# A planner that lengthens GpSimd and VectorE instructions beside each other, with a new load order, gates and ranks

## The chip, the cores and the metric

The kernel runs on one core of one Trainium2 chip. The metric is the device time of one execution in microseconds (us); lower is better. The kernel before took 287.44 us in the median of four runs (285.84 to 288.22). Besides, one execution was profiled; it took 286.84 us, of which the profile's span covers 284.9 us.

The engines appear in the profile as PE (TensorE matmuls), PEld (TensorE weight loads), DVE (VectorE), ACT (ScalarE), POOL (GpSimd) and SP (SyncE, which issues nearly all DMAs).

## The reference

Two layers follow each other. The first is a linear attention with a decaying state, over 4 batches, 8 heads, 768 steps and a head dimension of 48:

```python
for t in range(S):
    cur = np.einsum('bhd,bhe->bhde', u[None] * kt, vt)
    y[:, :, t] = np.einsum('bhd,bhde->bhe', rt, state + cur)
    state = w[None, :, :, None] * state + np.einsum('bhd,bhe->bhde', kt, vt)
```

Its result, reshaped to 3072 rows of 384, goes through a mixture of four experts, all of them computed for each row and weighted by normalised probabilities:

```python
for e in range(E):                       # 4 experts, 384 -> 1024 -> 384
    h = np.maximum(x @ w1[e], 0.0)
    out += p[:, e:e + 1] * (h @ w2[e])
```

## The kernel before

**Chunks and super-chunks.** The sequence is cut into chunks of 128 steps, 6 for each of the 4 batches, 24 in all, numbered `ci` with the batch running fastest. Four chunks (one of each batch) make a super-chunk `sc`, so there are six. A chunk's attention becomes a 128x128 masked product for each head (`At`, `mask`), a product with V (`Y`), a term of the state carried from the chunk before of the same batch, and an update of that state (`Sm`, `Sv`, `S`).

**The work of one chunk.** Three loads (`Rt`, `Kt`, `Vt`, 192 KB each, L232) go into one of four input buffers (`inp`). VectorE scales R and K by powers of the decay (`scale`, L397 from chunk 8 on). GpSimd multiplies R, K and u (`ruk_a`, L409, and `ruk_b`, L417), VectorE reduces that to a coefficient (`dcoef`, L430), and GpSimd multiplies V by it (`dv`, L435). A buffer comes free when scale, ruk_a, the cast of V and dv are done. From chunk 8 on, two DMA transposes per pair of chunks (L442) bring the scaled tile to the layout that TensorE wants; Y and dv are added on VectorE (`Yout`, L571); the state update is an add on VectorE (`Sv`, L638) and two half products on GpSimd (`S`, L648).

**The experts.** Super-chunks 0 and 1 go through eight slots `(expert, super-chunk, single)`: first layer (L701 or L707) into PSUM, relu on ScalarE (L716, L718), second layer (L738), weighted addition (L747, L749). For super-chunks 2 to 5, ScalarE scales the attention's result by each expert's probability first (`Xs`, L591) and DMA transposes it (L601); all four experts' first layers run (L707), and their hidden activations form one product of 2x2 blocks that is computed with seven block products (`P`, L905) in place of eight. This needs sums of the weight blocks (`mix`, L818) once, and sums of activation blocks (`sum`, L874) for each pair of chunks; products are collected by ScalarE copies (L932) and VectorE additions (`C`, L934). The mixes are computed once, after the two scaled super-chunks are through.

**The order.** Nothing is scheduled on the chip. While the program is built, a planner in Python plays the execution through. Every job has an engine, a duration, the jobs it needs, tokens that it takes and gives back (buffers), and a rank. Whenever an engine is free, the planner starts the ready job with the lowest rank. The order in which jobs start becomes the order of instructions in each engine's queue. The chip runs each queue strictly in that order, with semaphores for the dependences; the planner's times are thus not executed, only its order. Loads are SP jobs, ranked by their place in the list `ORDER`; one that has no free buffer is passed over for the next.

**What the change touches.** `GATES` (L140) names for each pair of chunks from 8 on an event before which it may not be scaled: a number below 8 is the first matmul of that slot, 8 to 11 the first matmul of an expert's first layer in super-chunk 2, 12 to 15 one of its block products, and from 16 on the same for super-chunk 3. `MIX_RANK`, `XS_RANK` and `SUM_RANK` shift the ranks of mixes, Xs and sums. `SLOWER` multiplies planned durations after the planner's 85th microsecond, by engine, for all but sum, Xs, mix and scale. `SHARED` lengthens a VectorE sum, scale, mix or Xs by 0.6 of the time for which GpSimd is still busy when it starts. `TAIL` is the time between an instruction's end and the start of one that waits for it.

Of the kernel before, what the change touches and what calls it, by code (L numbers as in the profile page):

```python
# [19 lines left out]
def kernel(  # L20
# [14 lines left out]
    B, H, S, D = r.shape  # L35
    HD = H * D
    C = 128
    NCH = S // C
    TOTC = B * NCH
    SUB = B  # L40
# [81 lines left out]
    for b in range(B):  # L122
# [14 lines left out]

    GATES = [3, 5, 8, 8, 16, 17, 7, 23]  # L140
    WARM, NSPIN = 6.6, 6
    TAIL = {"T": 0.27, "V": 0.17, "A": 0.20, "P": 0.17, "S": 0.0}
    DMAT = 8
# [6 lines left out]
    FIRST = 2  # L150
    SCALED = 2
    ONTO = {6: 1, 5: 6, 3: 5, 4: 7}
    MIX_RANK = 16.0
    XS_ON = {'A': 0.61}
    MIX_ON = {'V': 0.97}
    SCALE_US = 0.97
    VB_ON = {'A': 0.42, 'P': 0.5}
    XS_RANK = 0
    SUM_RANK = -60
    EARLY_SUM = 0.0  # L160
    NSH = 4
    SEQ_S = (((1, 0), (3, 0), (2, 0), (1, 1), (3, 1), (2, 1), (4, 0), (4, 1)),
             ((1, 2), (3, 2), (2, 2), (4, 2)))
    LATE, SLOWER = 85.0, {"V": 1.13, "P": 1.06, "A": 1.15}
    SHARED = 0.6
    SLOTS += [(e, sc, 0) for sc in range(2, SCALED) for e in range(E)]
    ORDER_P = (1, 2, 6, 7, 4, 5, 3)
    SEQ_P = ((0, 1, 0), (0, 2, 0), (0, 7, 0), (0, 1, 1), (0, 2, 1), (0, 7, 1), (0, 6, 0), (0, 6, 1), (0, 4, 0),
# [13 lines left out]
    def job(name, on, run, needs=(), rank=0.0, takes=(), drops=(), moves=None,  # L182
            behind=()):
        j = Job()
        j.behind = behind
        j.name, j.on, j.run, j.needs, j.rank = name, on, run, list(needs), rank
        j.takes, j.drops, j.moves = takes, drops, moves
        for k in drops:
            tokens[k] = tokens.get(k, 0) + 1
        j.pad = 0.0  # L190
        ci = name[1] if isinstance(name, tuple) and name[0] in ATT else -1
        if ci >= SUB:

            j.pad = PAD_PE if "T" in on else PAD
        j.no = len(jobs)
        assert name not in jobs
        jobs[name] = j
# [61 lines left out]
    def load_p():  # L259
# [1 line left out]
            prow, moe_domain_probs.rearrange("(n p) e -> n p e", p=C)))  # L261

    ORDER = ("K0 K1 R0 R2 R1 V0 K2 w1e0.1 w1e0.0 w1e0.2 V1 K3 V2 R3 w2e0.0 V3 w2e0.1 w2e0.2 p K4 w1e1.1 "
# [3 lines left out]
             " ".join(f"c{i}" for i in range(14, TOTC))).split()  # L267
    for what in ORDER:
        if what == "p":
            load_p()  # L270
# [93 lines left out]
    def attention(ci):  # L364
        b, c = ci % B, ci // B
# [3 lines left out]
        rk = float(ci)  # L369
        on_pe = -20.0 + 0.01 * ci  # L370
        pre = [("S", ci - NRK), ("T", ci - NRK, 1)] if ci >= NRK else []
        if ci >= 2 * SUB:

            g = GATES[(ci - 2 * SUB) // 2]
            if g < len(SLOTS):
                pre.append(("l1", *SLOTS[g][:2], 0, 0))
            else:
                i, g = divmod(g - len(SLOTS), 8)
# [16 lines left out]
        us = 0.48 if ci < SUB else 0.65  # L395
# [188 lines left out]
        elif dmat:  # L584
            n_p = b * NCH + c

            def xs(e):
                def run(eng):
                    o = y_e[:, e * HD:(e + 1) * HD]
                    if eng == "A":  # L590
                        nc.scalar.mul(o, tl["Ysb", ci], p_nat[:, e, n_p:n_p + 1])  # L591
                    else:
                        nc.vector.tensor_scalar(o, tl["Ysb", ci], scalar1=p_nat[:, e, n_p:n_p + 1],
                                                scalar2=None, op0=ALU.mult)
                return run
            for e in range(E):
                job(("Xs", ci, e), XS_ON, xs(e), [("Yout", ci)] + all_cast, rk + XS_RANK,
                    ((f"Yse{e // 2}", ci),) if e % 2 == 0 else (), (("dv", ci),),
# [54 lines left out]
        if c == 0:  # L653
            job(("S", ci), {"V": 0.56}, sv, [("Sm", ci), ("Yout", SUB - 1)], rk + 2, (), (("ys", "S", ci),))
        else:
            job(("Sv", ci), {"V": 0.5}, sv, [("Sm", ci)], rk - 0.1, (("Tn", ci),), (("ys", "S", ci),))
            job(("S", ci), {"P": 1.3}, sp, [("Sv", ci)], rk - 0.5, (), (("Tn", ci),))

    y_sb = weights.tile([128, 3 * HD], BF16)
    y_free, y_at = [0, 1, 2], {}  # L660
# [136 lines left out]
    def mix(what, hf):  # L797
# [28 lines left out]
        if not where:  # L826
            needs += [("l2", e, ci) for ci in range(SCALED * SUB) for e in (2 * hf, 2 * hf + 1)]
            needs += [("l2s", ci, e) for ci in range(SCALED * SUB, FIRST * SUB) for e in (2 * hf, 2 * hf + 1)]
        job(("mix", what, hf), MIX_ON, run, needs, MIX_RANK, ((where, "mix", home),) if where else ())

# [14 lines left out]
    def products(sc, q, at0):  # L845
# [21 lines left out]
        def sum_job(k, hf):  # L867
# [10 lines left out]
            if k in (2, 4):  # L878
                needs += [("P", sc, q, 1 if k == 2 else 2, h) for h in hs]
            job(("sum", sc, q, k, hf), {"V": 1.23 if hf == 2 else 0.7}, run, needs,  # L880
                at_of[{1: 6, 3: 6, 2: 6, 4: 3}[k]] + (EARLY_SUM if k in (1, 3) and not q and not hf else SUM_RANK), tuple(s_tok[h] for h in hs) if k == 1 else (),
                tuple(x for h in hs for x in hts[h]) + (tuple(s_tok[h] for h in hs) if k in (1, 2) else ()),
# [121 lines left out]
    avail = {"T": 3.7, "V": 4.5, "A": 3.3, "P": 1.5, "S": 0.6}  # L1004
# [25 lines left out]
    events = []  # L1030
    started = []
    gone = set()
    unknown = {n: len(q) for n, q in left.items()}
    known = {n: 0.0 for n in left}
    soon = {e: [] for e in avail}
# [2 lines left out]
    def offer(j):  # L1038
        for e in j.on:
            heapq.heappush(waiting[e], (j.rank, j.no, j))  # L1040
# [5 lines left out]
    now, seq, n_done = 0.0, 1, 0  # L1046
# [7 lines left out]
    def start(e):  # L1054

        nonlocal seq
        put_back, got = [], None
        while waiting[e]:
            it = heapq.heappop(waiting[e])
            j = it[2]  # L1060
            if j.name in gone:
                continue
            if ready_at[j.name] <= now + 1e-9 and \
                    fits(j) and \
                    not (j.moves and queued and queued[-1][1] > now + BACKLOG):
                got = j
                break
            put_back.append(it)
        for it in put_back:
            heapq.heappush(waiting[e], it)  # L1070
        if got is not None and now < HURRY:

            us = got.on[e]
            for i in soon[e]:
                if i.name not in gone and i.rank < got.rank and fits(i) and                         now < known[i.name] < now + 0.6 * us:
                    heapq.heappush(waiting[e], (got.rank, got.no, got))
                    heapq.heappush(events, (known[i.name], seq, "eng", e))
                    seq += 1
                    return False
        if got is None:  # L1080
            return False
        j = got
        gone.add(j.name)
        for t in j.takes:
            if t not in held:
                held.add(t)
                free[t[0]] -= 1
        us = j.on[e] * (2.0 if e == "T" and now < WARM and j.name not in ("wmm", "umm") else 1.0)
        if e in SLOWER and now > LATE and j.name[0] not in ("sum", "Xs", "mix", "scale"):
            us *= SLOWER[e]  # L1090
        if e == "V" and now > LATE and j.name[0] in ("sum", "scale", "mix", "Xs"):
            us += SHARED * min(us, max(0.0, avail["P"] - now))
        if j.moves:
            taken, end = dma(now, us, *j.moves)
            us = taken - now + 0.04
        started.append((now, len(started), e, j))
        avail[e] = now + us
        if not j.moves:
            end = now + us + TAIL[e]
        heapq.heappush(events, (avail[e], seq, "eng", e))  # L1100
        heapq.heappush(events, (end, seq + 1, "done", j))
        for u2 in users.get(j.name, ()):
            unknown[u2.name] -= 1
            known[u2.name] = max(known[u2.name], end)
            if not unknown[u2.name] and end < HURRY + 5:
                for e2 in u2.on:
                    soon[e2].append(u2)
        seq += 2
        return True

    while n_done < len(jobs):
        assert events, "no job can begin"
        now, _, what, x = heapq.heappop(events)
        batch = [(what, x)]
        while events and events[0][0] <= now + 1e-9:
            _, _, what, x = heapq.heappop(events)
            batch.append((what, x))
        for what, x in batch:
            if what == "done":
                n_done += 1  # L1120
                for t in x.drops:
                    count[t] -= 1
                    if count[t] == 0:
                        free[t[0]] += 1
                for u2 in users.get(x.name, ()):
                    left[u2.name].discard(x.name)
                    if not left[u2.name]:
                        ready_at[u2.name] = now + u2.pad
                        offer(u2)
                        if u2.pad:  # L1130
                            for e2 in u2.on:
                                heapq.heappush(events, (now + u2.pad, seq, "eng", e2))
                                seq += 1
        for e in avail:
            if avail[e] <= now + 1e-9:
                start(e)
# [49 lines left out]
```

## Time and profile before

| What | Value |
|---|---|
| median of four runs | 287.44 us |
| lowest, highest | 285.84, 288.22 us |
| the profiled execution, its span | 286.84 us, 284.9 us |
| TensorE busy with matmuls | 277.5 us (97%) |
| ScalarE, VectorE, GpSimd busy | 186.8, 179.3, 106.2 us |
| sums, mixes and scales of two chunks' R and K on VectorE (L874, L818, L397) | 45.4 + 7.5 + 16.6 us |
| GpSimd: ruk_a and ruk_b, dv, S | 27.1 + 25.6, 21.8, 22.0 us |
| HBM read, written | 26.79 MB, 4.72 MB |

A busy time is the union of an engine's instructions. Matmuls are pipelined: a 128x512 one is shown as 379 ns long, and the next one's start tells the true pace. An engine's idle time costs nothing unless what it does next ends on the path to the last store.

### The profile page before, as it was taken

What the parts mean: (1) busy time and instruction counts of PE and PEld (TensorE: products, weight loads), DVE (VectorE), ACT (ScalarE), POOL (GpSimd) and SP (SyncE); (2) the same over time, 40 slices, a digit from 0 to 9 for tenths busy, and PEclk for the clock granted to TensorE, in tenths of its full rate; (3) what the DMA queues carried; (4) which work ended last, traced back from release to release, by engine and by line L of the source; (5) the groups of instructions that cost most, each with busy time, mean ns of one, the idle gap of its engine ahead of it and who ended that gap; (6) DMA issues with size and microseconds to landing.
All of it is one profiled execution on the core that took longest, in us unless ns stands there. A gap on an engine that the chain in (4) does not pass through costs nothing.

```text
span 284.9 us, 6660 instructions
## 1 busy us (share of the span) xinstructions
PE 277.5 (97%) x2656; PEld 192.6 (68%) x2677; DVE 179.3 (63%) x289; ACT 186.8 (66%) x344; POOL 106.2 (37%) x126
## 2 busy tenths in 40 slices
PE   8989999999999999999999999999999999999995
PEld 3777555865774665445899445899644799444995
DVE  5867976579749665998687547898433473010761
ACT  4785968745748584888656788853699840899110
POOL 2872443661996655026158154667010000000000
PEclk9999999999999999999999999999999999999999
DMA  7999899889997988895475895896831241100011
GB/s 155 297 238 336 234 344 247 202 260 229 204 199 143 177 191 149 208 198 102 83 146 124 190 188 114 84 204 117 127 66 28 57 100 40 58 0 0 2 69 44
DMA packets 130290, 42.43 MB, mean 149 GB/s; under 512 B 118458, under 2 KB 130236, under 8 KB 130260
## 3 DMA queue, kind: packets, MB, share of 16 engines
q1 hardware_dynamic: 130100, 41.96, 66.9%
q8 instruction: 21, 0.34, 0.5%
q14 instruction: 9, 0.07, 0.1%
q10 hardware_dynamic: 160, 0.05, 0.1%
HBM read 26.79 MB, written 4.72 MB: 111 GB/s over the span
## 4 chain that ended last, share of the span: by engine, by line
PE 75%; DMA 10%; DVE 4%; SPq 4%; issue 2%; POOL 2%; ACT 1%; ACTq 0%; POOLq 0%; DVEq 0%
PE hT_ps L707 34%; PE M_ps L905 23%; PE out_ps L738 9%; SPq L232 4%; DMA RKin<-in_r_dram 3%; DMA stg<-in_moe_w_dram 3%; DMA RKin<-in_k_dram 3%; PE hT_ps L701 2%; DMA stg<-stg 2%; PE Y_ps L556 1%; PE At_all L509 1%; PE St_ps L629 1%; PE Y_ps L549 1%; DVE RK_sb L397 1%; SPq L246 1%
## 5 line engine op out<-in xcount | busy, mean ns | idle before, releaser
L718 ACT ACTIVATE hAll<-hT_ps 128x512 bf16<-128x512 f32 x168 | 98.6, 597 | 20.8 <-PE hT_ps L707 13.3
L707 PE MATMUL hT_ps<-stg,w_sb 128*128 128x512 bf16 x372 | 85.2, 379 | 0.6
L707 PEld LDWEIGHTS <-w_sb 128*128 128x128 bf16 x504 | 47.2, 98 | 52.2 <-DVE w_sb L80 0.3
L905 PEld LDWEIGHTS <-hAll 128*128 128x128 bf16 x768 | 63.1, 98 | 0.9 <-DVE hAll L874 0.3
L409 POOL TENSOR_TENSOR ruk<-RKin 128x384 f32<-128x384 f32 x24 | 27.1, 1129 | 53.8 <-DMA RKin<-in_k_dram 26.3
L738 PE MATMUL out_ps<-w_sb,hAll 128*128 128x384 bf16 x256 | 45.9, 326 | 0.0
L591 ACT ACTIVATE stg<-dv,p_nat 128x384 bf16<-128x384 f32 x64 | 36.4, 608 | 5.9 <-DMA stg<-stg 5.6
L905 PE MATMUL M_ps<-w_sb,hAll 128*128 128x192 bf16 x384 | 35.3, 246 | 0.0
L932 ACT COPY o_sb<-M_ps 128x192 f32<-128x192 f32 x31 | 9.8, 317 | 37.9 <-PE M_ps L905 37.0
L738 PEld LDWEIGHTS <-hAll 128*128 128x128 bf16 x256 | 23.9, 98 | 15.0
L435 POOL TENSOR_TENSOR dv<-Vt,dcoef 128x384 f32<-128x384 f32 x24 | 21.8, 910 | 26.7 <-ACT stg L591 25.1
L707 PE MATMUL hT_ps<-xTe,w_sb 128*128 128x512 bf16 x111 | 28.2, 379 | 0.4
L417 POOL TENSOR_TENSOR ruk<-ruk,U_sd 128x384 f32<-128x384 f32 x23 | 25.6, 1117 | 1.3
L648 POOL TENSOR_TENSOR S<-Tn,wC 64x192 bf16<-64x192 f32 x32 | 22.0, 687 | 6.3 <-DVE Tn L638 3.6
L874 DVE TENSOR_TENSOR hAll<-stg,hAll 128x1024 bf16<-128x1024 bf16 (+1 forms) x12 | 11.2, 932 | 20.0 <-PE M_ps L905 19.4
L874 DVE TENSOR_TENSOR hAll<-hAll 128x1024 bf16<-128x1024 bf16 (+1 forms) x24 | 22.8, 965 | 0.2
L749 DVE SCALAR_TENSOR_TENSOR o_sb<-out_ps,p_nat,o_sb 128x384 f32<-128x384 f32 x24 | 14.6, 616 | 12.5 <-PE out_ps L738 12.4
L701 PE MATMUL hT_ps<-xTe,w_sb 128*128 128x128 bf16 x288 | 18.7, 219 | 0.4 <-ACT w_sb L78 0.4
L934 DVE TENSOR_TENSOR o_sb<-o_sb,M_ps 128x192 f32<-128x192 f32 x24 | 8.4, 351 | 16.9 <-issue 10.3
L874 DVE TENSOR_TENSOR stg<-hAll 128x1024 bf16<-128x1024 bf16 (+1 forms) x12 | 11.4, 946 | 11.9 <-ACT hAll L718 11.9
L905 PE MATMUL M_ps<-w_mix,hAll 128*128 128x192 bf16 x192 | 18.6, 246 | 0.0
L905 PE MATMUL M_ps<-o_sb,hAll 128*128 128x192 bf16 x192 | 18.0, 246 | 0.1
(89 smaller groups left out, 311.3 us busy)
## 6 DMA issues: line engine op xcount, KB each, us to landing
stg<-in_moe_w_dram SPq DMA_DIRECT2D x16, 576.0 KB, 7.1
RKin<-in_k_dram SPq DMA_DIRECT2D x24, 192.0 KB, 4.1
RKin<-in_r_dram SPq DMA_DIRECT2D x24, 192.0 KB, 3.7
Vt<-in_v_dram SPq DMA_DIRECT2D x24, 192.0 KB, 4.3
out_dram<-o_sb SPq DMA_DIRECT2D x23, 192.0 KB, 2.0
stg<-in_moe_w_dram SPq DMA_DIRECT2D x8, 384.0 KB, 6.0
stg<-stg SPq DMA_TRANSPOSE x32, 2.8
RKT<-RK_sb SPq DMA_TRANSPOSE x16, 3.6
```

Of the source, the lines that this page charges most:

```text
L409: nc.gpsimd.tensor_mul(tl["ruk", ci], tl["Rt", ci], tl["Kt", ci])
L417: nc.gpsimd.tensor_mul(tl["ruk", ci], tl["ruk", ci], U_sd)
L435: nc.gpsimd.tensor_mul(tl["dv", ci], tl["Vt", ci], tl["dcoef", ci].to_broadcast((128, H, D)))
L591: nc.scalar.mul(o, tl["Ysb", ci], p_nat[:, e, n_p:n_p + 1])
L648: nc.gpsimd.tensor_mul(S_new[pr, :, cl], Tn2[pr, tn_at[ci], :, cl], wC[pr, :, None].to_broadcast((P2, NP, D)))
L701: nc.tensor.matmul(ps[:, i, :], w1_sb[:, e, db, (fb + i) * 128:(fb + i + 1) * 128], xTe[:, db, s0, :], start=(i == 0 and db == 0), stop=(i ...
L707: nc.tensor.matmul(ps[:, 0:n, :].rearrange("p a b -> p (a b)"), w1_sb[:, e, db, fb * 128:(fb + 1) * 128], xTe[:, x0 + db, s0:s0 + n, :].re ...
L718: nc.scalar.activation(hTs[:, fb, s0:s0 + n, :], ps[:, 0:n, :], AF.Relu)
L738: nc.tensor.matmul(ps, relu_tile(e, sc)[:, fb, s, :], w2_sb[:, e, fb, :], start=(fb == 0), stop=(fb == NFB - 1))
L749: nc.vector.scalar_tensor_tensor(oacc(ci), in0=tl["o", e, ci], scalar=pe, in1=oacc(ci), op0=ALU.mult, op1=ALU.add)
L874: nc.vector.tensor_tensor(o, x, y, op=op)
L905: nc.tensor.matmul(tl["P", sc, q, m], st, moving(m, hf, n), start=(hf == 0 and n == 0 and m not in ONTO), stop=(hf == 1 and n == 7), skip_ ...
```

## The change

The planner's durations change in four places, and the values that steer its order change with them.

- The one-sided term `SHARED = 0.6` becomes two-sided. Whenever a GpSimd instruction starts while a VectorE sum, mix or scale runs, or the other way round, the planner works out how long both will run beside each other, lengthens the starting one by its share (0.4 for VectorE, 0.5 for GpSimd) of that time, and lengthens the running one likewise, postponing its end. Xs is no longer among the instructions that this concerns.
- The factor 1.06 for GpSimd after 85 us goes.
- The state update `S` on GpSimd is planned with 1.1 us in place of 1.3 from chunk 8 on.
- The C additions and copies release what waits for them 0.15 us earlier in the plan.
- `GATES`, `MIX_RANK`, `XS_RANK` and `SUM_RANK` get new values, and `ORDER` is new from the 25th load on, now listing loads up to chunk 18 one by one.

No instruction is added or removed.

```diff
-    GATES = [3, 5, 8, 8, 16, 17, 7, 23]
+    GATES = [0, 2, 7, 8, 16, 16, 13, 0]
...
-    MIX_RANK = 16.0
+    MIX_RANK = 27.25
...
-    XS_RANK = 0
-    SUM_RANK = -60
+    XS_RANK = 6.75
+    SUM_RANK = -91.5
...
-    LATE, SLOWER = 85.0, {"V": 1.13, "P": 1.06, "A": 1.15}
-    SHARED = 0.6
+    LATE, SLOWER = 85.0, {"V": 1.13, "A": 1.15}
+    SHARED = {"V": 0.4, "P": 0.5}
...
-             "w1e1.0 R4 w2e1.0 w1e1.2 K5 R5 w2e1.1 w2e1.2 w1e2.1 V4 w1e2.2 w1e2.0 V5 w2e2.2 V7 K7 w2e2.1 "
-             "V6 K6 V8 R6 R7 w2e2.0 w1e3.2 w1e3.1 w1e3.0 K8 V10 K10 w2e3.0 V11 R8 K9 R11 R9 R10 V9 w2e3.2 "
-             "K11 V13 w2e3.1 K13 R12 V12 K12 R13 " +
-             " ".join(f"c{i}" for i in range(14, TOTC))).split()
+             "w1e1.0 R4 w2e1.0 w2e1.1 w1e1.2 K5 w1e2.2 w2e1.2 R5 V4 w1e2.1 w1e2.0 R14 V5 V6 w2e2.2 w2e2.1 "
+             "R7 V8 V7 R10 K10 K11 V11 K9 R13 V9 R17 K17 K7 V17 R12 R11 V13 K6 K15 R9 w2e2.0 R18 R6 R15 "
+             "w2e3.2 V16 w1e3.2 w2e3.0 w1e3.1 V14 V15 V10 K8 w2e3.1 V12 K14 R16 K16 w1e3.0 K12 R8 K13 K18 "
+             "V18 " +
+             " ".join(f"c{i}" for i in range(19, TOTC))).split()
...
-            job(("S", ci), {"P": 1.3}, sp, [("Sv", ci)], rk - 0.5, (), (("Tn", ci),))
+            job(("S", ci), {"P": 1.3 if ci < 2 * SUB else 1.1}, sp, [("Sv", ci)], rk - 0.5, (), (("Tn", ci),))
...
+    on_port = {}
+    ONE_PORT = ("sum", "mix", "scale")
...
-        if e in SLOWER and now > LATE and j.name[0] not in ("sum", "Xs", "mix", "scale"):
+        if e in SLOWER and now > LATE and j.name[0] not in ONE_PORT and j.name[0] != "Xs":
             us *= SLOWER[e]
-        if e == "V" and now > LATE and j.name[0] in ("sum", "scale", "mix", "Xs"):
-            us += SHARED * min(us, max(0.0, avail["P"] - now))
+        on_port[e] = j
+        if now > LATE and (e == "P" or e == "V" and j.name[0] in ONE_PORT):
+            o = "V" if e == "P" else "P"
+            if avail[o] > now + 1e-9 and (o == "P" or on_port[o].name[0] in ONE_PORT):
+                both = min(us / (1 - SHARED[e]), (avail[o] - now) / (1 - SHARED[o]))
+                us += SHARED[e] * both
+                more = SHARED[o] * both
+                on_port[o].late += more
+                avail[o] += more
+                heapq.heappush(events, (avail[o], seq, "eng", o))
+                seq += 1
...
-            end = now + us + TAIL[e]
+            end = now + us + TAIL[e] - (0.15 if j.name[0] in ("C", "D") else 0.0)
...
-            if what == "done":
+            if what == "done" and x.late:
+                heapq.heappush(events, (now + x.late, seq, "done", x))
+                seq += 1
+                x.late = 0.0
+            elif what == "done":
```

More of the change, by code (lines that the diff above doesn't have):

```diff
@@ L189, in job @@
             tokens[k] = tokens.get(k, 0) + 1
-        j.pad = 0.0
+        j.pad = j.late = 0.0
         ci = name[1] if isinstance(name, tuple) and name[0] in ATT else -1
```

## The prediction

> **What bounds the kernel now.** I read the page's engine shares first, then the busy time in stretches of 10 us, then the chain that ended last, and only then VectorE and GpSimd. The engine shares and the slices:
>
> ```profile
> PE 277.5 (97%) x2656; PEld 192.6 (68%) x2677; DVE 179.3 (63%) x289; ACT 186.8 (66%) x344; POOL 106.2 (37%) x126
> PE   8989999999999999999999999999999999999995
> DMA  7999899889997988895475895896831241100011
> ```
>
> TensorE is busy 277.5 of 284.9 us; no other engine passes 66%. The stretches (length, then busy time and count of PE, PEld, DVE, ACT, POOL, the granted clock, DMA share, GB/s) show where the other 7.4 us lie:
>
> ```profile
> 0.00:10.00 10.00, 8.41 (x77) 4.95 (x78) 7.05 (x25) 5.69 (x11) 4.16 (x13) 1.00 0.84 180
> 10.00:20.00 10.00, 8.92 (x148) 7.26 (x147) 7.39 (x15) 7.04 (x14) 8.51 (x10) 1.00 0.97 265
> ...
> 90.00:100.00 10.00, 9.77 (x83) 5.67 (x84) 7.43 (x13) 6.30 (x13) 6.05 (x8) 1.00 1.08 176
> ...
> 180.00:190.00 10.00, 9.75 (x127) 9.30 (x126) 8.60 (x13) 5.75 (x14) 5.31 (x6) 1.00 1.10 162
> ```
>
> The first 20 us hold 1.59 + 1.08 = 2.7 us of it, and about 3.2 us follow the last matmul. That leaves 7.4 - 2.7 - 3.2 = 1.5 us for the 262 us between, and the two worst stretches there lack 0.23 and 0.25 us. The busy time is modelled and could hide stalls, so I checked it on the chain, in order of time (start, length, what):
>
> ```profile
> 89.22 1.75 DVE RK_sb L397
> 90.97 0.48 DVE dv L571
> 91.45 0.04 issue
> 91.49 0.33 PE Y_ps L549 x4
> ...
> 242.80 10.96 PE hT_ps L707 x50
> 253.76 0.05 issue
> 253.81 9.44 PE hT_ps L707 x43
> 263.25 18.50 PE M_ps L905 x224
> 281.75 0.02 issue
> 281.77 0.27 DVE o_last L927
> ```
>
> From 242.8 us on the chain is matmuls end to end: 18.50 / 224 = 82.6 ns for each of the 192-column ones, 10.96 / 50 = 219 ns for each of the 512-column ones. The same pitches hold in the middle: starts of successive L707 matmuls lie 215 to 216 ns apart almost everywhere. Comparing every start with the pitch of its kind, I find one stall over 0.2 us after the 20th microsecond: 0.29 us at 91.2 us, before the Y matmuls of the chain above. There the chain leaves TensorE and runs back through VectorE, GpSimd and input loads to 53 us. So TensorE is full, but around 91 us only just.
>
> The Trainium skill ("Perfetto Trace Analysis", Identifying the Most-Contended Engine) calls matmul busy time a bad measure of headroom and prefers the share of weight loading. That share is 68% here, which by the rule would leave some 90 us to gain; the sum below goes by the start-to-start pitches instead, and they show no such gap.
>
> **The change, part by part.** It adds and removes no instruction: same matmuls, vector work and bytes. It alters the planner's durations and thus the order in which each queue is written out.
>
> *The contention terms.* Here is the thing modelled, VectorE and then GpSimd:
>
> ```profile
> 146.32 1.97 DVE L874 TENSOR_TENSOR hAll<-hAll 128x2048 bf16<-128x2048 bf16 x1
> 150.88 1.25 DVE L874 TENSOR_TENSOR hAll<-hAll 128x2048 bf16<-128x2048 bf16 x1
> ```
> ```profile
> 146.22 1.00 POOL L409 TENSOR_TENSOR ruk<-RKin 128x384 f32<-128x384 f32 x1 [1.02 <-DMA RKin<-in_k_dram]
> 147.29 1.86 POOL L417 TENSOR_TENSOR ruk<-ruk,U_sd 128x384 f32<-128x384 f32 x1
> 150.22 0.83 POOL L435 TENSOR_TENSOR dv<-Vt,dcoef 128x384 f32<-128x384 f32 x1 [1.07 <-ACT stg L591]
> ```
>
> A sum that takes 1.22 us alone takes 1.97; a product of 1.00 us takes 1.86. Adding up every GpSimd instruction after 85 us: they exceed their undisturbed durations by 8.9 us, and 8.88 of it falls on the 25 that overlap a sum, mix or scale of VectorE, by 19.2 us together: 0.46 us per us beside each other, where the new planner says 0.5. The same overlap costs VectorE 5.9 us, 0.31 per us, where the new planner says 0.4 and the old one, for VectorE alone, 0.6. An undisturbed pair of state updates (L648) takes 1.08 us; the new entry is 1.1, the old was 1.3 x 1.06 = 1.38. So the new durations are nearer to the chip. Their direct worth: even if all 8.9 + 5.9 us went, TensorE waits after a VectorE or GpSimd instruction for 0.3 us only. I price this part at -0.3 us, with 0 and -1.5 us (every idle microsecond found above) as ends.
>
> The row and a rule part here. In the row, the L409 product that began 0.10 us ahead of the sum is not lengthened, and the sum is, by 0.75 us. The Trainium skill ("SBUF — State Buffer", SBUF: two separate sides) says that the pair of ports is an exclusive lock: who starts first keeps it, the other blocks. By that rule lengthening both is wrong for each single instruction, and the written order can be wrong by some 0.8 us in places; by proportional shares it is right. Neither alters the sum, since VectorE and GpSimd are covered by TensorE's queue.
>
> *The loads from the 25th on.* The first 24 are the same, issued until about 26 us, so the first 20 us keep their 2.7 us of idle time and their warming matmuls. After that the list puts R14 before V5, and weights of experts 2 and 3 later. The list is only a priority: a load without a free input buffer is passed over. But R14 takes one of four input buffers at some 40 us and keeps it until the scale of chunk 14, which waits (gate 8, as before) for the first matmuls of super-chunk 2, at 114.2 us now. In the run before, chunk 14's loads were issued at some 85 to 93 us. Hence between 40 and 85 us chunks 6 to 13 have three buffers. With the present holding times (from the issue of the first load, in SyncE's timeline, to the end of dv, in GpSimd's: about 15, 21, 29, 15, 29 and 31 us for chunks 6 to 11, 140 us together in the 55 us from 40 to 95) they need 140 / 55 = 2.5 on average. Three suffice on average, not in every moment. The three loads pulled forward, 192 KB each, take 0.97 us apiece at the 202 GB/s that 50 to 100 us average, 2.9 us together, in a stretch whose DMA share is 0.9 to 1.1. Cost: 0 where TensorE has other ready matmuls (it has the second-layer blocks of eight slots to choose from), +2.9 us where they fall on the chain at 85 to 91 us; a gain of at most the 0.29 us stall. I take 0, because today's chain with the same loads costs only 0.29.
>
> *Gates and ranks.* Chunks 8 to 11 and 20 to 23 may be scaled earlier, so GpSimd and VectorE get some work earlier. The mixes fall from rank 16 to 27.25, behind all chunk work. Now all eight run at 114.8 to 125.3 us, alone, at 0.95 us. Their first reader on TensorE starts at 138.9 us, so there are 13 us of cover. VectorE has 20.3 us of work in the 23.0 us from 114.8 to 137.8; if the 6.3 us that GpSimd works there all fell beside mixes, 6.3 x 0.31 = 2.0 us come on top, and 22.3 still fit. Cost 0, up to +2 us if they don't. Rank of the sums from -60 to -91.5: they now go ahead of C additions (about 0.35 us each) with which they compete; 0, ends -0.3 and +0.5.
>
> **The sum.** The profiled execution took 286.84 us, with its span of 284.9; the median of the four runs is 287.44, 0.6 above. Against the profiled one: -0.3 + 0 + 0 = 286.5. The same -0.3 on the median gives 287.1, my forecast.
>
> **The rivals.**
>
> *Slower: the fourth buffer.* Chunk 14 holds a buffer, one of chunks 8 to 11 gets its loads when another's dv ends (75 to 95 us), and super-chunk 2 is not transposed when its first layer should begin at 114 us. For it: the chain at 53 to 91 us already runs through those loads. Against it: 2.5 of 3 buffers on average. It decides once the last of chunks 8 to 11 is scaled over 10 us later than now (91 us), as 23 us lie between that and 114.2. Price: from 2.9 us to about 6 (a chunk is held 15 us at least, less 10 of slack, plus about 1 for contention), 290 to 293.5.
>
> *Slower: late mixes or gates.* VectorE passes 23 us before 137.8 and the products wait: +2 to +4 us, 289.5 to 291.5.
>
> *Faster.* The slowest of the four runs is 2.4 us above the fastest. If that is stalls around 91 us that the profile missed, the change may end them: 285.5. More than 1% needs 2.9 us, and only 1.5 are idle in all.
>
> *It does nothing.* VectorE and GpSimd overlap as much as before, only the plan knows it: 287.4, hardly to be told from the forecast.
>
> **How the numbers follow.** Within 1% (about what a measurement of this kernel can tell from no change), 284.6 to 290.3: 0.74, made of the forecast (0.40), the change that does nothing (0.18), stalls of under 2.9 us (0.12) and the mild gain (0.04). Slower by over 1%: 0.21, made of the buffer (0.14) and late mixes or gates (0.07). Faster by over 1%: 0.05, for idle time that I have misread. The forecast's own range is 285.8 to 288.5. The range for 8 in 10 is 285.3 (all 1.5 us gone from 287.44, and the spread of a median) to 290.8, well into the slower cases.
>
> **What the profile after would show.** TensorE between 20 and 281 us idle by under 1.5 us again, last matmul at 281 to 282 us: forecast right. Less lengthening of L409 to L648 after 85 us without a shorter span: contention was covered. TensorE gaps between 85 and 120 us behind loads, L397 or L591: the buffer. Gaps at 138 to 146 us behind L818: the mixes. I am wrong upward if the work that TensorE can turn to in 85 to 115 us is shorter than I think, and downward if a start-to-start pitch hides a wait.

## Result and the profile after

The changed kernel takes 286.31 us in the median of 46 runs (285.5 to 289.95), the kernel before 287.07 us in 70 runs. The ratio is 0.9978 with a 95% interval of 0.9969 to 0.9987: by the ratio 0.6 us faster (0.4 to 0.9). Its profiled execution took 285.5 us, with a span of 283.5, against 286.84 and 284.9 before.

In the changed kernel's file the lines behind the list `ORDER`, which is one line longer, lie one further down: what was L707 is L708, L905 is L906, L874 is L875, and so on. The engine shares on the page of the changed kernel:

```profile
PE 276.8 (98%) x2654; PEld 192.8 (68%) x2677; DVE 178.0 (63%) x289; ACT 186.0 (66%) x343; POOL 108.2 (38%) x127
```

TensorE has the same work and a smaller idle rest. Two stretches of 10 us of the changed kernel, in the same columns as before:

```profile
90.00:100.00 10.00, 9.95 (x85) 5.67 (x84) 6.67 (x11) 7.58 (x15) 6.14 (x10) 1.00 0.96 146
...
180.00:190.00 10.00, 10.00 (x126) 10.00 (x124) 8.07 (x12) 5.98 (x15) 3.72 (x4) 1.00 0.63 123
```

The two worst stretches of before, 9.77 at 90 us and 9.75 at 180 us, are now 9.95 and 10.00. The end of the chain of the changed kernel, in order of time (start, length, what):

```profile
241.41 10.96 PE hT_ps L708 x50
...
252.41 9.44 PE hT_ps L708 x43
261.86 18.49 PE M_ps L906 x224
```

These last three groups of matmuls have the lengths they had before, 10.96, 9.44 and 18.5 us; they begin 1.39 us earlier. So nothing was won after 242 us. Of the 1.4 us, 0.21 were there at 30 us already: the first 512-column matmul of the experts starts at 30.37 us in place of 30.58, with the same TensorE instructions before it. The other 1.19 us were won between, from 30.4 us to the last matmul: 249.72 us in place of 250.91. I use this length from here on and call it the **steady part**.

Where they were won can't be read from TensorE's busy time, since a shown duration outlasts the pitch (246 ns against 82.5 for a product), and only in part from matmul starts, since some matmul records are missing (2656 and 2654 are left). The weight loads are complete: 2677 in every profile, as many as the matmuls in the two profiles that miss none (h1 and g1, below). In those two a weight load starts, in the median, 2 ns after the matmul before it. Between successive weight loads, the kernel before has five gaps over what their kinds need elsewhere: 0.29 us at 91.0, 0.35 at 140.7, 0.25 at 150.4, 0.37 at 187.8 and 0.11 at 197.5 us (times of the last load ahead of the gap), 1.37 us together. The changed kernel has one, 0.11 us at 132.9. Two of the five in the timeline of weight loads of the kernel before (start, length, line, count, idle time in front and who ended it):

```profile
137.57 3.26 PEld L905 LDWEIGHTS <-hAll 128*128 128x128 bf16 x40
141.16 3.25 PEld L905 LDWEIGHTS <-hAll 128*128 128x128 bf16 x40 [0.33 <-DVE hAll L874]
...
150.75 0.20 PEld L629 LDWEIGHTS <-RK_sb 128*128 128x128 bf16 x4 [0.23 <-DVE Tn L638]
```

The first waits for a sum, the second for the addition of a state (`Tn`), which on VectorE stands behind a sum that takes 1.75 us in place of 1.22:

```profile
148.48 1.75 DVE L874 TENSOR_TENSOR hAll<-stg,hAll 128x2048 bf16<-128x2048 bf16 x1
150.16 0.54 DVE L638 TENSOR_TENSOR Tn<-S,St_ps 128x384 f32<-128x384 bf16 x1
```

In the stretch around the first, the changed kernel has:

```profile
137.08 1.94 PEld L906 LDWEIGHTS <-hAll 128*128 128x128 bf16 x24
139.00 0.27 PEld L550 LDWEIGHTS <-RKT 128*128 128x128 bf16 x4
139.21 0.29 PEld L557 LDWEIGHTS <-AtM 128*128 128x128 bf16 x8
139.43 4.58 PEld L906 LDWEIGHTS <-hAll 128*128 128x128 bf16 x56
```

Nothing waits. A chunk's Y matmuls, 0.4 us of TensorE, now stand among the products ahead of the one that needs the late sum. VectorE's and GpSimd's timelines show why the sum of the first gap, the second line of each, was late before. The kernel before, VectorE, then GpSimd:

```profile
139.06 1.32 DVE L874 TENSOR_TENSOR stg<-hAll 128x1024 bf16<-128x1024 bf16 x1
140.42 0.69 DVE L874 TENSOR_TENSOR hAll<-hAll 128x1024 bf16<-128x1024 bf16 x1
```
```profile
138.60 1.24 POOL L435 TENSOR_TENSOR dv<-Vt,dcoef 128x384 f32<-128x384 f32 x1 [5.14 <-ACT stg L591]
```

The changed kernel, VectorE, then GpSimd:

```profile
138.82 0.68 DVE L875 TENSOR_TENSOR stg<-hAll 128x1024 bf16<-128x1024 bf16 x1
139.53 0.69 DVE L875 TENSOR_TENSOR hAll<-hAll 128x1024 bf16<-128x1024 bf16 x1
```
```profile
137.52 0.83 POOL L436 TENSOR_TENSOR dv<-Vt,dcoef 128x384 f32<-128x384 f32 x1 [1.53 <-ACT stg L592]
```

Before, a `dv` of GpSimd lay beside the sum ahead of it, which took 1.32 us in place of 0.68. Now that `dv` ends before this one begins. Over the whole run after 85 us, though, the engines overlap no less: 20.1 us in place of 19.2. GpSimd is lengthened more, by 11.4 us in place of 8.9, and VectorE less, by 4.3 in place of 5.9. A second profile of each (f5 and f4) says the same: 10.8 in place of 8.7, and 5.2 in place of 6.7.

### The profile page after: what moved, and what is told of

Its sections match the earlier page's. It is cut to its first block, busy times and chain, and to the rows that moved or that the text cites. A ratio compares the mean times of both kernels' runs of the same rounds, so it can differ in the third digit from the quotient of the medians.

```text
span 283.5 us, 6644 instructions
## 1 busy us (share of the span) xinstructions
PE 276.8 (98%) x2654; PEld 192.8 (68%) x2677; DVE 178.0 (63%) x289; ACT 186.0 (66%) x343; POOL 108.2 (38%) x127
## 4 chain that ended last, share of the span: by engine, by line
PE 92%; SPq 3%; DMA 3%; issue 1%; DVE 1%; POOL 0%; ACT 0%; ACTq 0%
PE hT_ps L708 38%; PE M_ps L906 26%; PE out_ps L739 15%; PE hT_ps L702 5%; DMA RKin<-in_k_dram 3%; SPq L232 2%; PE At_all L510 2%; PE Y_ps L557 1%; PE St_ps L630 1%; PE Y_ps L550 1%; PE RKT_ps L462 1%; PE At_ps L510 1%; SPq L246 1%; POOL RK_sb L393 0%; PE xT_ps L614 0%
## 5 line engine op out<-in xcount | busy, mean ns | idle before, releaser
L719 ACT ACTIVATE hAll<-hT_ps 128x512 bf16<-128x512 f32 x168 | 98.3, 597 | 30.4 <-PE hT_ps L708 25.0
L708 PE MATMUL hT_ps<-stg,w_sb 128*128 128x512 bf16 x370 | 85.4, 379 | 0.7
L708 PEld LDWEIGHTS <-w_sb 128*128 128x128 bf16 x504 | 47.1, 98 | 52.1 <-DVE w_sb L80 0.3
L906 PEld LDWEIGHTS <-hAll 128*128 128x128 bf16 x768 | 63.4, 98 | 0.7
L592 ACT ACTIVATE stg<-dv,p_nat 128x384 bf16<-128x384 f32 x64 | 37.1, 610 | 7.6 <-DMA stg<-stg 7.2
L436 POOL TENSOR_TENSOR dv<-Vt,dcoef 128x384 f32<-128x384 f32 x24 | 24.4, 1017 | 38.7 <-ACT stg L592 32.9
L906 PE MATMUL M_ps<-w_sb,hAll 128*128 128x192 bf16 x384 | 35.1, 246 | 0.0
L708 PE MATMUL hT_ps<-xTe,w_sb 128*128 128x512 bf16 x111 | 28.1, 380 | 0.5
L418 POOL TENSOR_TENSOR ruk<-ruk,U_sd 128x384 f32<-128x384 f32 x23 | 26.6, 1157 | 1.0
L649 POOL TENSOR_TENSOR S<-Tn,wC 64x192 bf16<-64x192 f32 x32 | 19.9, 620 | 14.1 <-DVE Tn L639 12.7
L875 DVE TENSOR_TENSOR hAll<-hAll 128x1024 bf16<-128x1024 bf16 (+1 forms) x24 | 22.4, 946 | 3.1 <-PE M_ps L906 2.9
L875 DVE TENSOR_TENSOR hAll<-stg,hAll 128x1024 bf16<-128x1024 bf16 (+1 forms) x12 | 11.2, 934 | 14.7 <-PE M_ps L906 14.1
L906 PE MATMUL M_ps<-w_mix,hAll 128*128 128x192 bf16 x192 | 18.5, 246 | 0.0
L875 DVE TENSOR_TENSOR stg<-hAll 128x1024 bf16<-128x1024 bf16 (+1 forms) x12 | 10.4, 868 | 12.4 <-ACT hAll L719 12.4
L527 DVE TENSOR_TENSOR AtM<-At_all,mask 128x1024 bf16<-128x1024 f32 x8 | 9.8, 1222 | 13.1 <-PE At_all L510 13.1
```

The lines of the kernel that those rows point to most:

```text
L418: nc.gpsimd.tensor_mul(tl["ruk", ci], tl["ruk", ci], U_sd)
L436: nc.gpsimd.tensor_mul(tl["dv", ci], tl["Vt", ci], tl["dcoef", ci].to_broadcast((128, H, D)))
L649: nc.gpsimd.tensor_mul(S_new[pr, :, cl], Tn2[pr, tn_at[ci], :, cl], wC[pr, :, None].to_broadcast((P2, NP, D)))
L708: nc.tensor.matmul(ps[:, 0:n, :].rearrange("p a b -> p (a b)"), w1_sb[:, e, db, fb * 128:(fb + 1) * 128], xTe[:, x0 + db, s0:s0 + n, :].re ...
L719: nc.scalar.activation(hTs[:, fb, s0:s0 + n, :], ps[:, 0:n, :], AF.Relu)
L875: nc.vector.tensor_tensor(o, x, y, op=op)
```

## The experiments

Theory A: the planner's better durations bring the gain, because the order then fits what the chip does. Theory B: the new gates, ranks and loads bring it. A third question was whether contention or something else makes the stalls. In this table "steady part" is the time from the start of the first 512-column matmul of the experts to the start of the last matmul in the kernel's profile, and "start" the time of that first one. The ratio comes from the timed executions of a kernel, the other two columns from the single profiled one.

| Kernel | Ratio to before (95% interval) | Start, us | Steady part, us |
|---|---|---|---|
| before | 1 | 30.58 | 250.91 |
| f4_before_again | one run, 288.63 us | 32.16 | 251.13 |
| changed | 0.9978 (0.9969 to 0.9987) | 30.37 | 249.72 |
| f5_after_again | 0.9968 (0.9945 to 0.9990) | 30.99 | 249.70 |
| e1_durations_only | 0.9970 (0.9950 to 0.9991) | 31.71 | 249.69 |
| e2_steering_only | 0.9999 (0.9980 to 1.0019) | 30.54 | 250.53 |
| e3_light_pool | 0.9956 (0.9931 to 0.9980) | 31.26 | 249.91 |
| e4_old_loads | 1.0018 (0.9993 to 1.0043) | 30.78 | 250.70 |
| f1_share_only | 0.9994 (0.9971 to 1.0016) | 31.25 | 250.63 |
| f3_pool_costs_only | 1.0035 (1.0009 to 1.0060) | 32.56 | 251.59 |
| h1_after_light_pool | 0.9975 (0.9955 to 0.9995) | 31.62 | 249.69 |
| g1_probs_early | 0.9979 (0.9965 to 0.9993) | 31.28 | 249.69 |

### Durations alone

The changed kernel with `GATES`, `MIX_RANK`, `XS_RANK`, `SUM_RANK` and `ORDER` as before:

```diff
-    GATES = [0, 2, 7, 8, 16, 16, 13, 0]
+    GATES = [3, 5, 8, 8, 16, 17, 7, 23]
```

> The changed kernel's planner durations (two-sided sharing, no factor for GpSimd, state update 1.1, C released earlier), with the gates, ranks and load order of the kernel before. Theory A (the better durations bring the gain): ratio to the kernel before 0.9978, as the whole change, 0.6 us; the stalls of TensorE at 140.7, 150.4 and 187.8 us (0.35 + 0.25 + 0.37 us between weight loads) are gone. Theory B (gates, ranks and loads bring it): ratio 1.000 or above, those stalls remain or move.

Measured: 0.997 (0.995 to 0.9991) and a steady part of 249.69 us, in which no gap between weight loads exceeds what their kinds need by 0.1 us. That is what theory A forecast, and the whole gain; whether better durations bring such an order every time is another matter, which e4 below decides. How they act is seen best at the stall at 91 us. VectorE in the kernel before (the first line holds two scales):

```profile
87.93 3.04 DVE L397 TENSOR_TENSOR RK_sb<-RKin,W_both 128x768 bf16<-128x768 f32 x2
90.90 0.54 DVE L571 TENSOR_TENSOR dv<-Y_ps,dv 128x384 f32<-128x384 f32 x1
```

VectorE with the new durations alone:

```profile
89.06 1.70 DVE L397 TENSOR_TENSOR RK_sb<-RKin,W_both 128x768 bf16<-128x768 f32 x1
90.69 0.55 DVE L571 TENSOR_TENSOR dv<-Y_ps,dv 128x384 f32<-128x384 f32 x1
91.15 0.94 DVE L397 TENSOR_TENSOR RK_sb<-RKin,W_both 128x768 bf16<-128x768 f32 x1
```

An undisturbed scale takes 0.95 us. Beside GpSimd the two of before took 3.04 us together, and the addition to Y, for which TensorE's next Y matmuls wait, stood behind both. With the new durations the addition stands between the two, behind one lengthened scale and no longer behind two. The contention is still there, the first scale takes 1.70 us. What goes is TensorE's wait behind it.

### Steering alone

The kernel before with the changed `GATES`, `MIX_RANK`, `XS_RANK`, `SUM_RANK` and `ORDER`:

```diff
-    GATES = [3, 5, 8, 8, 16, 17, 7, 23]
+    GATES = [0, 2, 7, 8, 16, 16, 13, 0]
```

> The planner durations of the kernel before, with the changed gates, ranks and load order. Theory A: ratio 1.000 or worse (the new values were chosen under other durations, 0 to +3 us). Theory B: 0.998, 0.6 us faster, and TensorE without stalls over 0.2 us after 20 us.

Measured: 0.9999 (0.998 to 1.0019), no difference. The five gaps are gone here too, but a new one of 0.89 us stands in front of the first layer of super-chunk 2. The weight load there, with the steering alone:

```profile
114.48 1.41 PEld L708 LDWEIGHTS <-w_sb 128*128 128x128 bf16 x8 [0.96 <-DMA stg<-stg]
```

It waits for a transpose of ScalarE's scaled results. The new values alone bring no time, as theory A forecast. The profiled execution, at 286.29 us, is the fastest of the twelve, 1.5 us under their median, so its trace may not show what the others wait for.

### GpSimd made light, order kept

The kernel before, with most of GpSimd's products left out from chunk 8 on. Its file is longer, so that the sums of L874 stand in L883 here. ruk_a is treated like dv, and ruk_b and the state update work on 6 of 48 columns alone:

```diff
-            nc.gpsimd.tensor_mul(tl["dv", ci], tl["Vt", ci], ...)
+            nc.gpsimd.memset(tl["dv", ci], 0.0)
+            nc.gpsimd.tensor_mul(tl["dv", ci][:, :, 0:6], tl["Vt", ci][:, :, 0:6], ...)
```

> The order of the kernel before, with GpSimd's work from chunk 8 on cut: ruk_a and dv become a fill and a product of 6 of 48 columns, ruk_b and the state update work on 6 of 48 columns (so ruk, dv and the state are computed in part alone). It takes the contention away and leaves every queue's order. If contention makes the stalls at 140.7 and 150.4 us: they vanish, -0.6 us (ratio 0.998), while those at 91.0 and 187.8 us stay. If they have another cause: ratio 1.000, stalls in place.

Measured: 0.9956 (0.9931 to 0.998), and a steady part of 249.91 us. The gaps at 140.7 and 150.4 us are gone, as expected of contention; the one at 91.0 us is gone too, which I had not expected, and the one at 187.8 us is 0.10 us in place of 0.37. So 1.0 of the 1.2 us that the changed kernel won in the steady part goes with GpSimd's work.

GpSimd's own instructions are shorter here too, so this run alone doesn't separate contention from GpSimd's length. The rows above do, for three gaps: at 91.0, 140.7 and 150.4 us (0.89 us together) TensorE waits behind a lengthened scale or sum of VectorE. For the one at 187.8 us contention isn't shown: in the chain it stands behind a ScalarE copy, an Xs and a DMA transpose, and it is absent from a second profile of the unchanged kernel (f4 below). Nor is all contention gone: GpSimd is still lengthened by 7.0 us after 85 us, in place of 8.9, but VectorE by 0.1 in place of 5.9. What TensorE had waited for was the lengthening of VectorE.

The same was done to the changed kernel:

> The changed kernel with GpSimd's work from chunk 8 on cut to 6 of 48 columns, as in e3_light_pool (ruk, dv and the state are computed in part alone). If the changed order has put the contention where TensorE doesn't wait for it: 249.7 us from the first 512-column matmul to the last matmul, as without the cut (in the kernel before the cut brought 250.9 to 249.9), ratio to the kernel before 0.997. If contention still costs TensorE something: under 249.5 us and a ratio of 0.995 or less.

Measured: 0.9975 (0.9955 to 0.9995) and 249.69 us, against 249.72 and 249.70 in two profiles of the changed kernel. The changed kernel overlaps VectorE and GpSimd for 20.1 us, and within 0.03 us it costs TensorE nothing.

### Loads as before, the rest changed

The changed kernel with the `ORDER` of the kernel before, from the 25th load on:

```diff
-             "w1e1.0 R4 w2e1.0 w2e1.1 w1e1.2 K5 w1e2.2 w2e1.2 R5 V4 w1e2.1 w1e2.0 R14 V5 V6 w2e2.2 w2e2.1 "
...
+             "w1e1.0 R4 w2e1.0 w1e1.2 K5 R5 w2e1.1 w2e1.2 w1e2.1 V4 w1e2.2 w1e2.0 V5 w2e2.2 V7 K7 w2e2.1 "
...
```

> The changed kernel with the load order of the kernel before (chunk 14's R no longer early, weights of experts 2 and 3 earlier). If the held fourth buffer costs the changed kernel anything, this is faster than it: ratio to the kernel before under 0.997. If the loads only removed the 0.29 us stall at 91 us: ratio 0.999, TensorE stalls again by some 0.3 us between 80 and 100 us. If loads and the rest were chosen together: 1.000 or slower, with new stalls.

Measured: 1.0018 (0.9993 to 1.0043) and 250.70 us: the third of the three. The weight loads of this kernel, at 114 and at 142 us (two stretches):

```profile
114.24 1.64 PEld L707 LDWEIGHTS <-w_sb 128*128 128x128 bf16 x9 [0.49 <-issue]
...
142.06 3.00 PEld L905 LDWEIGHTS <-hAll 128*128 128x128 bf16 x36 [0.69 <-DVE hAll L874]
```

No stall between 80 and 100 us, but new ones of 0.42 and 0.70 us over the pitch elsewhere. The second is contention on TensorE's path again: the sum that it waits for takes 1.20 us, and the two ahead of it 1.02 and 0.99, where one takes 0.68 undisturbed. VectorE's last one and GpSimd beside it:

```profile
140.80 1.20 DVE L874 TENSOR_TENSOR hAll<-hAll 128x1024 bf16<-128x1024 bf16 x1
```
```profile
140.30 1.16 POOL L435 TENSOR_TENSOR dv<-Vt,dcoef 128x384 f32<-128x384 f32 x1
```

So the better durations don't ensure an order without such stalls. Of the three orders planned with all of them (changed, e1, e4) two have none, of the four planned without some of them (before, e2, f1, f3) each has at least one over 0.2 us; that is too few to tell knowledge from luck. The loads taken back alone cost what the whole had brought, although loads, gates and ranks taken back together (e1) cost nothing.

### The durations in two halves

The kernel before with the two-sided sharing alone (f1: the first pair of lines and the code behind it), and with GpSimd's durations alone (f3: the rest):

```diff
-    SHARED = 0.6
+    SHARED = {"V": 0.4, "P": 0.5}
...
-    LATE, SLOWER = 85.0, {"V": 1.13, "P": 1.06, "A": 1.15}
+    LATE, SLOWER = 85.0, {"V": 1.13, "A": 1.15}
-            job(("S", ci), {"P": 1.3}, ...)
+            job(("S", ci), {"P": 1.3 if ci < 2 * SUB else 1.1}, ...)
```

> The kernel before with the two-sided sharing term alone (GpSimd keeps its factor 1.06 and 1.3 us for the state update, C keeps its release). Theory A1 (knowing the contention brings the gain): like all durations together, ratio 0.997, and the time from the first 512-column matmul to the last matmul falls from 250.9 to 249.7 us. Theory A2 (the nearer base durations of GpSimd bring it): 1.000 and 250.5 us or more.

> The kernel before with GpSimd's new base durations alone (no factor 1.06, state update 1.1 us). Theory A1: ratio 1.000, first 512-column matmul to last matmul 250.5 us or more. Theory A2: 0.997 and 249.7 us.

Measured: 0.9994 (0.9971 to 1.0016) for the sharing alone and 1.0035 (1.0009 to 1.006) for GpSimd's durations alone, with steady parts of 250.63 and 251.59 us. Neither theory A1 nor A2 holds. The weight load behind the largest gap, with the sharing alone and then with GpSimd's durations alone:

```profile
197.45 1.25 PEld L905 LDWEIGHTS <-stg 128*128 128x128 bf16 x15 [0.87 <-issue]
```
```profile
201.72 1.25 PEld L905 LDWEIGHTS <-hAll 128*128 128x128 bf16 x15 [1.28 <-issue]
```

The sharing alone removes the four earlier gaps and leaves one of 0.89 us at 196.5; in the chain, ScalarE's copy that TensorE waits for there stands behind an Xs, and that Xs behind a DMA transpose. GpSimd's durations alone keep the gaps at 93 and 143 us (0.34 and 0.35) and add one of 1.29 us at 200 us, behind C additions of VectorE in the chain. I could not show more than that: whether these ends are luck of the order, or each half needs the other, is open. The earlier release of C was not run alone.

### The two kernels profiled again

> The kernel before, profiled once more, to see how far a profile repeats. If the stalls belong to the order: again five of them, at 91, 141, 150, 188 and 198 us, and 250.9 us from the first 512-column matmul to the last matmul, within 0.2. If they are accidents of one execution: other places, other sizes. The first 512-column matmul, which waits for the first loads, may move by 0.5 us or more.

> The changed kernel once more. Ratio 0.998; 249.7 us from the first 512-column matmul to the last matmul and no stall over 0.2 us in between, if that belongs to the order; the first 512-column matmul at 30.4 to 31.7 us.

The kernel before again: a steady part of 251.13 us (0.22 from the first profile, where 0.2 was expected at most), gaps at 92.6 (0.70 us), 142.7 (0.35), 152.4 (0.33) and 199.3 us (0.20). Three of its weight loads:

```profile
26.73 0.55 PEld L341 LDWEIGHTS p_ps<-hAll 24*128 24x128 f32 x4 [1.40 <-DVE S L642]
...
93.48 0.18 PEld L549 LDWEIGHTS <-RKT 128*128 128x128 bf16 x3 [0.82 <-issue]
...
143.16 3.25 PEld L905 LDWEIGHTS <-hAll 128*128 128x128 bf16 x40 [0.34 <-DVE hAll L874]
```

Four of five places repeat, with sizes that vary; the one at 188 us does not. The first line is another thing: the transposes of the probabilities wait 1.40 us, 1.08 of them over their pitch. It belongs to the start, which varies by 2 us between the profiles of this case (30.37 to 32.56 us), in kernels whose weight loads up to there are alike (351, in the same order). In the chain of this profile and of e1's, TensorE waits there for the load of the probabilities. The changed kernel again: 249.70 us, no gap over 0.1 us in the steady part, a start of 30.99 us, all as expected.

### A try at the start

The changed kernel with the probabilities' load at the start of ScalarE's queue:

```diff
+    nc.scalar.dma_start(prow, moe_domain_probs.rearrange("(n p) e -> n p e", p=C))
-        load_job("prow", (0.36, 2), lambda: nc.sync.dma_start(prow, ...))
+        load_job("prow", (0.36, 2), lambda: None)
```

> The changed kernel with the load of the probabilities (48 KB in small packets) issued from ScalarE's queue at the start and taken out of SyncE's, all queues otherwise in the same order. If the wait of the transposes of the probabilities at 25 us (0.6 us and 1.1 us in two profiles) costs the typical execution: it is gone, the first 512-column matmul starts at 30.4 us, ratio to the kernel before 0.995. If it is rare, or the early load delays the first loads: 0.998 or above.

Measured: 0.9979 (0.9965 to 0.9993), not to be told from the changed kernel. There is no wait at 25 us in its profile, but neither is there in the two profiles of the changed kernel; the 0.6 and 1.1 us of the expectation are those of e1 and f4. Its first 512-column matmul starts at 31.28 us, 0.91 later than in the changed kernel's first profile. In the chain of both, a transpose that waits about 0.5 us for a scaled tile leads back to the same load of K, which lands at 17.48 us here and at 16.57 there. Whether the early load delayed it, or it varies of itself, isn't shown. No version is clear of the changed kernel's interval on the faster side.

## Why the prediction was right, point by point

The forecast was 287.1 us from 287.44, that is -0.3 us; measured are -0.6 us (0.4 to 0.9). In absolute terms 286.31 us were measured, 0.8 below the forecast, and half of that is the base: the median of the kernel before is 287.07 us in 70 runs, not 287.44 as in the first four. The forecast's sign in the profile, a last matmul at 281 to 282 us, was missed: it ends at 280.3 us.

**TensorE is full, so little can be won or lost.** Right, and more strictly than I said. Four kernels (changed, e1, h1, g1) have a steady part of 249.69 to 249.72 us. As far as the gaps between weight loads show, that is the pace of the matmuls themselves, and in the kernel before it was exceeded by 1.2 us in 251.

**"One stall over 0.2 us after the 20th microsecond", "TensorE waits after a VectorE or GpSimd instruction for 0.3 us only".** This is the step that was mis-sized: -0.3 us, where the steady part shows -1.2. There were four stalls over 0.2 us. I compared matmul starts and took gaps of some pitches for missing records. Two of the stalls stand there as 0.36 us from start to start ahead of 141.16 us and 0.45 us ahead of 188.21 us, 4.3 and 5.4 product pitches of 82.5 ns, so not whole numbers. The stretch from 180 us, whose missing 0.25 us the prediction names, holds the second of them. The -1.5 us that I gave as an end came from busy time, where the product stalls show only in part, and held the 1.2 by luck. The group of product weight loads on the page of the kernel before had it in its last column (busy and mean ns, then idle before, releaser):

```profile
L905 PEld LDWEIGHTS <-hAll 128*128 128x128 bf16 x768 | 63.1, 98 | 0.9 <-DVE hAll L874 0.3
```

**"Neither alters the sum, since VectorE and GpSimd are covered by TensorE's queue."** Wrong in three places, right elsewhere: of 14.8 us of lengthening, about 0.9 us reached TensorE (the gaps at 91.0, 140.7 and 150.4 us; e3: 250.91 to 249.91). And it was not won by less overlap, but by an order that puts other work in the waits and short work ahead of lengthened work.

**Lock or shares.** The prediction's own row shows the case in which GpSimd begins first: its product at 146.22 us keeps its 1.00 us, and the sum that begins 0.10 us later is lengthened. e3 shows the other. GpSimd's timeline in that kernel, then VectorE's:

```profile
138.97 0.42 POOL L442 MEMSET dv<- 128x384 f32 x1 [6.07 <-ACT stg L600]
...
144.85 0.27 POOL L444 TENSOR_TENSOR dv<-Vt,dcoef 128x48 f32<-128x48 f32 x1
...
146.62 1.17 POOL L411 TENSOR_TENSOR ruk<-RKin 128x48 f32<-128x48 f32 x1 [1.15 <-DMA RKin<-in_k_dram]
```
```profile
138.84 0.69 DVE L883 TENSOR_TENSOR hAll<-stg,hAll 128x1024 bf16<-128x1024 bf16 x1 [1.96 <-PE M_ps L914]
...
146.43 1.22 DVE L883 TENSOR_TENSOR hAll<-hAll 128x2048 bf16<-128x2048 bf16 x1
```

A product of 6 of 48 columns takes about 0.3 us undisturbed and 1.17 us when it begins 0.19 us into a sum, which keeps its 1.22 us. All VectorE's sums and scales after 85 us together are lengthened by 0.1 us in this kernel. So the one that begins first goes through, and the other waits for its end, as the Trainium skill has it ("SBUF — State Buffer", SBUF: two separate sides). The planner's shares of 0.5 and 0.4 average over both orders, and the average itself depends on which engine begins first: 0.46 us of lengthening per us beside each other for GpSimd and 0.31 for VectorE before, 0.57 and 0.21 in the changed kernel. They were good enough to find an order without stalls, here and in e1, not in e4.

**The share of weight loading as headroom.** It is 68% in the changed kernel as it was before, while the steady part is at its floor; for this kernel the rule that I weighed says nothing of what can be won.

**The loads and the fourth buffer: 0, or slower.** The premise was right: R14 is issued at 37.8 us and keeps its buffer. The rival did not come: no stall between 45 and 132 us. Three buffers sufficed, as the average of 2.5 had suggested. The price of 0 holds for the whole; e4 shows that loads of another choice cost 1 us there.

**Mixes, gates and ranks: 0.** Right as a price, though the gates were misread in part: chunks 12, 13, 18 and 19 may be scaled earlier too, and chunks 20 and 21 later (7, the first matmul of the last slot, became 13, a block product of super-chunk 2). e1 without them has the same steady part as the whole. Seven of the eight mixes still run alone by 121.4 us; the last is at 130.25 us beside GpSimd and takes 1.28 us, without a reader waiting.

Open is why the timed gain is 0.6 us where the steady part shows 1.2. The start, which varies by 2 us from execution to execution, lies between, and the executions that were not profiled may stall less or elsewhere; they have no trace.

## What to carry to other kernels

Look for stalls of a full TensorE between its weight loads, whose records are complete, and not in its busy time. When an engine that is two thirds busy is lengthened now and then by another, the cost is what stands behind the lengthened instruction in a queue; a plan that knows the lengthening can put the urgent short instruction first, or other work into the wait, without any less contention. It need not succeed (e4). Values that steer such a plan belong together: the gates, ranks and loads alone brought nothing, and the old loads among the new values took the gain away.

## What the runs showed of the hardware

A fill by GpSimd, which reads nothing from SBUF, keeps its 0.42 us beside a sum (at 138.97 us above; 0.41 to 0.42 us in all 16 fills of ruk), while a product of 48 columns in total takes up to 1.32 us in place of 0.29 (at 147.87 us in e3). That a GpSimd instruction of 0.3 us can take four times its own length was a surprise, and that VectorE's sums keep theirs when they begin first. And the steady part repeats to 0.03 us in five profiles in which nothing waits, while the first 30 us vary by 2 us.
